# A transformer block's second-level stage: when its token operands are prepared at its start, and when the next stage's are loaded at its end

## The chip, the cores and the metric

The kernel runs on one core of a Trainium2 chip. The metric is the device time in microseconds (us) of one execution. Three executions of the kernel before took 2743.86, 2738.77 and 2740.04 us; their median is 2740.04 us.

## The reference

One sequence of 2048 tokens with 1024 features goes through an adaLN-conditioned block. Cut to its skeleton (all data is fp32):

```python
mod = (silu(c) @ w_mod) -> sa, ca, ga, sb, cb, gb      # 1024 values each
h = layernorm(x) * (1 + ca) + sa
x1 = x + ga * (infini_attention(h) @ wo)               # 32 heads, 4 segments of 512 tokens
h2 = layernorm(x1) * (1 + cb) + sb
out = x1 + gb * ((gelu(h2 @ w_gate) * (h2 @ w_up)) @ w_down)   # 1024 -> 3584 -> 1024
```

The change concerns the way from `x1` through `h2` into the two products `h2 @ w_gate` and `h2 @ w_up`.

## The kernel before

**Arithmetic.** TensorE multiplies fp32 data as pairs of rounded numbers: every operand is cut into a high part `hi` (copied by ScalarE, line 925) and a low part `lo = src - hi` (VectorE or GpSimd, line 922), and every product is three matmuls: hi by hi, hi by lo, lo by hi. One such cut of an operand therefore takes one instruction on ScalarE and one on VectorE, or one on ScalarE and two half-size ones on GpSimd.

**The feed-forward stages.** The two wide products are computed with two levels of Strassen-Winograd. The level that the change touches is the *second-level stage*, `two(n)` (from L1104, matmuls in L1123). It runs over 14 weight pairs, n = 0 to 13, which the text calls pair 0 to pair 13. For each pair it computes seven products, in the order `ROUND = (1, 6, 2, 7, 5, 4, 3)`, for i = 1 and for i = 2, which are the first and the second half of the 1024 features (called the first and the second half below). A product is six matmuls of 128 by 512, a pair 84. The products add up in PSUM in tiles `pa` (products 1 and 2), `pb` (6, 7, 4) and `pc` (5, 3); `pa` shares two PSUM buffers, and `pb` and `pc` share five. The evictions are `c<-pa` on ScalarE (L1133), `x<-pb`, `x<-pc` on VectorE for i = 1 and `y<-pb`, `y<-pc` for i = 2 (L1139, L1141), and GpSimd adds x to y. Pair 0 runs the seven products of i = 1 and then the seven of i = 2; all other pairs alternate i = 1 and i = 2 for each product. The results go to a DRAM tensor `st_d`, from which the next stage reads them back.

That next stage is `gate_up(m)` (L1350, 60 matmuls for each m): five more products for each of 28 chunks of the 3584 columns in a first pass over half of the tokens (m = 0 to 27) and in a second pass over the other half (m = 28 to 55). Its token operands `A{pass}_{product}_{kt}` are prepared by `a_next(p)` (L1180): ten loads `ra` of 512 KB each, two to a product, and four cuts to a product.

**Token operands of the second-level stage.** They are called `AA{i}_{r}_{c}`: half i, product r, chunk c (0 or 1). They come from `unit(i, c, p)`, a load `u` of 512 KB from the normalised tokens `h_d`, with p the group of tokens (p = 0 is segment 0, p = 1 is segment 2). `a_early` loads the units (1, 0, 0) and (1, 1, 0) early and prepares AA1_1 and AA1_2. `a_first` then waits until segment 2 is normalised, loads everything else, and prepares the rest: for each i, sums and differences of the units (s, u: L1016 to L1018 on VectorE, the difference `diff` on GpSimd), and then a cut for each product and chunk. For products 5 and 4 with c = 1, the low part is computed on GpSimd, for all others on VectorE. `a_first` loads the units (1, 0, 0) and (1, 1, 0) a second time, because `a_early` does not hand its tiles on. The units (2, 1, p) go to tiles of the T ring, which exists only once the projections' pools are closed (`pools(3)`); in the build the loads `units(2, 1)` are therefore issued when the last projections are done.

**What runs ahead of it.** The attention's output projection (L773, eviction `xr<-y` on VectorE, L777) runs in blocks of four token tiles; the last two, block (3,0) and block (3,1), stand right before pair 0. Between the matmuls of block (3,0) TensorE transposes segment 2's normalised tokens (L269, `tpb<-ident,nb`), four tiles of 128 tokens, two steps for each. `norm_steps` spaces these: for four token tiles or fewer, a tile's statistics come 4 steps after its load, its scaling (L248 on ScalarE) after 6 and its transposes after 9, and a new tile starts every 4 steps.

**Order and queues.** For TensorE, VectorE, ScalarE and GpSimd the order in this part of the kernel is that of the program: generators ("sides") are stepped between the products, so each engine's instructions stand in the order in which the code issues them, and each engine works through its list in that order. SyncE (SP) issues nearly all DMAs, in an order set by a scheduler, and it too works in order: a DMA that waits for its buffer holds up those behind it.

**Rings in SBUF that matter.** `raw` has 4 buffers (weights of a pair, units, g and u weights of the next stage), `ra` 2, `T` 5 (the x outputs of a pair, some units, some `ra` loads), `g` 3 (the y outputs).

**The end of the stage.** At pair 13, `a_next(0)` is started as a side: it issues five loads (three to T buffers, two to `ra` buffers), then prepares one operand after another, each after the product of pair 13 that frees the operand's place. The third and each later step first issues one more load, to an `ra` buffer. Beside it runs `b_part(0)`, which prepares the weights of m = 0. `gu_load(1)`, the weights of m = 1 (`rg1`, `ru1`), is issued after product 4 of i = 2 of pair 13. At m = 27, `a_next(1)` does the same for the second pass.

## Time and profile before

The profiled execution took 2744.0 us; its span, the time from the first to the last instruction, is 2742.3 us.

| what | us |
|---|---|
| median of three executions | 2740.04 |
| the profiled execution | 2744.0 |
| its span | 2742.3 |
| TensorE busy in the span | 2677.0 (98 %) |
| pair 0 (1121.2 to 1160.5) | 39.3 |
| pair 1 (1160.5 to 1183.3) | 22.8 |
| pair 13 (1397.9 to 1428.8) | 30.9 |
| m = 0 (1428.8 to 1449.5) | 20.7 |

In the rows of the profile, times are in us from the span's start. "DVE" is VectorE, "ACT" ScalarE, "POOL" GpSimd, "PE" TensorE, "SPq" the queue of SyncE. A row gives start, duration, engine, source line, operation, output and inputs, and in square brackets the idle time before it on its engine and what ended that. The difference between the time of a pair and that of its 84 matmuls when nothing holds them up is time in which TensorE waits or runs at a lower clock.

### The profile page before, as it was taken

The numbers are of one execution on the slowest core, as the hardware profiler recorded it, in microseconds if no ns is written. First come the engines' busy times: TensorE is split into PE (matmuls) and PEld (weight loads), VectorE is DVE, ScalarE is ACT, GpSimd is POOL, SyncE is SP. The second block draws the span as 40 slices with busy tenths as digits, with TensorE's granted clock in tenths as the row PEclk, the third lists the DMA queues.
The fourth block names the chain that finished last, engine by engine and source line by source line (L and its number), as shares of the span: only waits on it lengthen the run. The fifth ranks groups of instructions, "written<-read, shape, count | busy, mean of one in ns | idle before, by whom it ended". The sixth has DMA issues, their size and how long they took to land.

```text
span 2742.3 us, 42592 instructions
## 1 busy us (share of the span) xinstructions
PE 2677.0 (98%) x14068; PEld 2227.6 (81%) x14068; DVE 1753.4 (64%) x3746; ACT 1261.3 (46%) x2924; POOL 1066.2 (39%) x1646
## 2 busy tenths in 40 slices
PE   7999999999999999899989999999999999999999
PEld 6898888888888787678867888878888888888887
DVE  7677667776766745577766655567666654575456
ACT  6778776767676634354442222232222233233323
POOL 4333334433333532365648777736565300000000
PEclk9999999999999999899999999999999999999999
DMA  7455535444434577366769988789999897795563
GB/s 261 112 158 143 134 113 162 120 129 141 131 101 135 175 236 234 125 219 208 249 210 356 335 276 270 264 287 370 370 373 367 332 332 237 262 307 198 183 207 125
DMA packets 266188, 613.37 MB, mean 224 GB/s; under 512 B 26992, under 2 KB 51568, under 8 KB 265968
## 3 DMA queue, kind: packets, MB, share of 16 engines
q1 hardware_dynamic: 265968, 610.66, 66.7%
q8 instruction: 111, 1.82, 0.3%
q14 instruction: 109, 0.89, 0.1%
HBM read 372.53 MB, written 187.70 MB: 204 GB/s over the span
## 4 chain that ended last, share of the span: by engine, by line
PE 52%; DMA 3%; DVE 3%; POOL 1%; issue 1%; ACT 1%; SPq 0%; DVEq 0%; POOLq 0%; ACTq 0%
PE f L1350 25%; PE y L1550 19%; PE pb L1123 3%; PE pc L1123 2%; PE pa L1123 2%; DMA rm<-h_d 1%; DVE A L922 1%; DMA ra<-mix_d 1%; DMA X<-hid_d 0%; DMA u<-h_d 0%; DMA wr<-gd_d 0%; POOL y L922 0%; DMA ru<-wu 0%; DVE AA L922 0%; DMA mix_d<-rm 0%
## 5 line engine op out<-in xcount | busy, mean ns | idle before, releaser
L1350 PE MATMUL f<-A,B 128*128 128x512 f32 x3360 | 766.0, 391 | 8.9 <-ACT B L925 3.8
L1350 PEld LDWEIGHTS f<-A,B 128*128 128x128 f32 x3360 | 631.7, 188 | 142.8 <-ACT B L925 6.8
L1550 PE MATMUL y<-B,L 128*128 128x512 f32 x2352 | 533.9, 390 | 0.6 <-DVE L L922 0.3
L1550 PEld LDWEIGHTS y<-B,L 128*128 128x128 f32 x2352 | 441.6, 188 | 92.6 <-ACT L L925 0.7
L611 ACT ACTIVATE sj<-sj,mm 128x384 f32<-128x384 f32 (+3 forms) x512 | 281.1, 552 | 40.2 <-DVE mm L609 39.6
L698 POOL TENSOR_SCALAR_AFFINE_SELECT pt<-pt 128x128 f32<-128x128 f32 x512 | 166.8, 347 | 332.3 <-ACT pt L697 324.3
L609 DVE CUSTOM_DVE_ANT_0 sj<-S,mask 128x384 f32<-128x384 f32 (+3 forms) x512 | 228.2, 488 | 97.0 <-PE S L607 70.7
L697 ACT ACTIVATE pt<-T 128x256 f32<-128x256 f32 (+3 forms) x512 | 182.3, 444 | 132.4 <-PE T L695 126.0
L1376 ACT ACTIVATE g<-g 128x512 f32<-128x512 f32 x56 | 35.4, 633 | 415.7 <-DVE g L1375 402.1
L925 ACT ACTIVATE L<-X 128x512 fp32r<-128x512 f32 x168 | 105.8, 630 | 257.3 <-PE y L1550 165.6
L922 DVE TENSOR_TENSOR L<-X,L 128x512 fp32r<-128x512 f32 x168 | 115.9, 691 | 145.7 <-ACT L L925 145.7
L386 POOL TENSOR_TENSOR w<-r,w 128x256 fp32r<-128x256 f32 x180 | 133.2, 771 | 141.5 <-ACT w L380 141.5
L395 PE MATMUL kv<-w,hha 128*128 128x256 f32 x896 | 175.2, 287 | 2.2 <-DVE vx L413 2.2
L1264 POOL TENSOR_TENSOR rw<-rw,gbb 128x256 f32<-128x256 f32 x112 | 109.2, 1009 | 155.9 <-DMA rw<-wd 150.6
L1123 PE MATMUL pb<-AA,BB 128*128 128x512 f32 x504 | 129.9, 406 | 20.2 <-DVE x L1139 15.4
L395 PEld LDWEIGHTS kv<-w,hha 128*128 128x128 f32 x896 | 145.3, 193 | 3.4 <-DVE vx L413 2.5
L1123 PEld LDWEIGHTS pb<-AA,BB 128*128 128x128 f32 x504 | 97.5, 196 | 44.5 <-DVE x L1139 18.0
L773 PE MATMUL y<-wo,hho 128*128 128x512 f32 x384 | 127.8, 396 | 0.2 <-DVE xr L777 0.2
L395 PE MATMUL kv<-w,hla 128*128 128x256 f32 x448 | 127.5, 285 | 0.0
L695 PE MATMUL T<-qs,ks 128*128 128x256 f32 (+3 forms) x512 | 105.7, 327 | 1.8 <-DVE ry L674 1.1
L607 PE MATMUL S<-ks,qs 96*128 96x384 f32 (+3 forms) x512 | 106.9, 330 | 0.3
L925 ACT ACTIVATE B<-t 128x512 fp32r<-128x512 f32 x84 | 49.7, 622 | 121.4 <-POOL t L922 121.4
(283 smaller groups left out, 5179.2 us busy)
## 6 DMA issues: line engine op xcount, KB each, us to landing
B<-wc_d SPq DMA_DIRECT2D x112, 512.0 KB, 3.4
cg<-st_d SPq DMA_DIRECT2D x112, 256.0 KB, 6.6
hid_d<-g SPq DMA_DIRECT2D x56, 512.0 KB, 4.5
wc_d<-T SPq DMA_DIRECT2D x56, 512.0 KB, 6.5
X<-hid_d SPq DMA_DIRECT2D x112, 256.0 KB, 4.9
bc_d<-B SPq DMA_DIRECT2D x54, 512.0 KB, 6.1
B<-bc_d SPq DMA_DIRECT2D x54, 512.0 KB, 7.1
wr<-gd_d SPq DMA_DIRECT2D x84, 256.0 KB, 4.1
```

The lines of the kernel that those rows point to most:

```text
L386: nc.gpsimd.tensor_sub(w[:, 1, c], r[:, c], f32(w[:, 0, c]))
L395: nc.tensor.matmul(ps, b[:, sl], w[:, a], start=(kt == 0 and a == 0 and b is hi), stop=(kt == KT - 1 and a == 1), **kw)
L609: nc.vector.tensor_tensor_reduce(out=sj[:, :nv], in0=ps[:, :nv], in1=mask[:, L - nv:], scale=-1.0, scalar=3.4e38, op0=ALU.add, op1=ALU.min ...
L611: nc.scalar.activation(sj[:, :nv], sj[:, :nv], AF.Exp, bias=mm[:, j, i:i + 1], scale=-1.0, accum_out=ll[:, i, j:j + 1])
L697: nc.scalar.activation(pt, ps[:, nn - n:nn], AF.Exp)
L698: nc.gpsimd.affine_select(pt[:, :P], pt[:, :P], pattern=[[1, P]], compare_op=ALU.is_ge, fill=0.0, base=0, channel_multiplier=-1)
L773: nc.tensor.matmul(ps, b[:, i * P:(i + 1) * P], w[:, a, g % 2], start=(g == 0 and a == 0 and b is hi), stop=(g == G - 1 and a == 1))
L922: f(*xs)
L925: nc.scalar.activation(hi, src, AF.Copy)
L1123: nc.tensor.matmul(ps, w[:, a, at:at + P], A["a", i, r, k][b], start=(r in (1, 6, 5) and k == a == b == 0), stop=(k == 1 and a == 1), skip ...
L1350: nc.tensor.matmul(ps, B[m, i][:, a, kt * P:(kt + 1) * P], A[p, i, kt][b], start=(start and kt == 0 and a == 0 and b == 0), stop=(kt == 3 ...
L1550: nc.tensor.matmul(banks[t], ops[k][:, y, t * P:(t + 1) * P], B[slots[k]][:, x], start=(i not in (2, 4, 3) and j == 0 and x == 0 and y == ...
```

## The change

It has five parts.

1. **`norm_steps`** for four tiles or fewer (segment 2 alone): statistics, scaling and transposes come 6, 8 and 13 steps after the load, before 4, 6 and 9.
2. **The early units are kept.** `a_early` stores its tiles in `ts`, and `a_first` uses them: two loads of 512 KB less.
3. **Order in `a_first`.** Before, it went through half 1, and then through half 2 with both chunks of each product together. Now, after half 1, it prepares chunk 0 of half 2 alone; chunk 1 waits until product 4 of i = 1 of pair 0 has been issued (`ff["half"]`). The difference of units (2, 1, p) moves from GpSimd to VectorE.
4. **Exit.** `a_next(0)` starts at pair 12, before at pair 13, with seven loads ahead, before five; the sixth and seventh go to `raw` buffers, the last three to T buffers. It is also stepped ahead of `b_part(0)`. `gu_load(1)` is issued from `a_next` at its eighth operand.
5. **Pass boundary.** In `a_next(1)`, five steps pass ahead of the ninth operand, the first of product 4.

```diff
-        period, at_stat, at_scale, at_turn = (5, 5, 7, 10) if len(toks) > 4 else (4, 4, 6, 9)
+        period, at_stat, at_scale, at_turn = (5, 5, 7, 10) if len(toks) > 4 else (4, 6, 8, 13)
...
-            ts = [unit(1, c, 0, raw_tile) for c in range(2)]
+            for c in range(2):
+                ts[1, c] = [unit(1, c, 0, raw_tile)]
...
             for c in range(2):
-                units(1, c)
-            units(2, 0)
+                ts[1, c].append(unit(1, c, 1, raw_tile))
+            units(0, ra_tile)
...
+            for c in range(2):
+                summed(1, c)
+                yield
+            for r in (6, 7, 5, 4, 3):
+                for c in range(2):
+                    put(1, r, c)
                     yield
...
+            put(2, 1, 0)
+            yield
+            summed(2, 0)
+            yield
+            for r in ROUND[1:]:
+                if r == 5:
+                    while (2, 1) not in ts:
                         yield
+                put(2, r, 0)
+                yield
+            while not ff.get("half"):
+                yield
+            put(2, 1, 1)
+            yield
+            summed(2, 1, nc.vector)
+            yield
+            for r in ROUND[1:]:
+                put(2, r, 1)
+                yield
...
+                if n == 0 and (i, r) == (1, 4):
+                    ff["half"] = True
...
-                    gu_load(1)
...
+            T_tile = lambda n: pair_tile(n, "T", 5)
+            homes = [T_tile] * 3 + [ra_tile] * 2 + [raw_tile] * 2 + [T_tile] * 3 if p == 0 else (
+                [raw_tile] * 2 + [ra_tile]) * 3 + [raw_tile]
...
-            for _ in range(5):
+            for _ in range(5 if p else 7):
                 load()
...
-                if q > 1:
+                if q > p:
                     load()
+                if p == 0 and q == 7:
+                    gu_load(1)
                 while (("a", 2, ROUND[q // 2]) if p == 0 else (FC - 1, i)) not in done:
+                    yield
+                for _ in range(5 if (p, q) == (1, 8) else 0):
                     yield
...
-        units(2, 1)
+        units(1, lambda n: pair_tile(n, "T", 5))
...
             elif n:
+                sides.append([b_part(0), 1, "b"])
+            if n == NJ - 2:
                 flush("m")
                 following = a_next(0)
-                sides.append([b_part(0), 1, "b"])
                 sides.append([following, 2])
```

**VectorE at the start of the stage.** In these rows `xr2<-y3_1_k` are the evictions of the last projection block's tiles, `AA` the low parts of the token operands, `u2_1_0` the unit of half 2 and chunk 1, and `x0_1<-pb0_1` the first eviction of pair 0. Before:

```order
L777 TENSOR_TENSOR xr2_14586<-y3_1_1_14658,xr2_14586 128x512
L1033 TENSOR_TENSOR u1_1_0_14607<-u1_1_0_14607 128x512
L922 TENSOR_TENSOR AA1_3_1_1_14714<-u1_1_0_14607,AA1_3_1_0_14713 128x512
L777 TENSOR_TENSOR xr2_14586<-y3_1_2_14718,xr2_14586 128x512
L777 TENSOR_TENSOR xr2_14586<-y3_1_3_14745,xr2_14586 128x512
L922 TENSOR_TENSOR AA2_1_0_1_14796<-u2_0_0_14611,AA2_1_0_0_14795 128x512
L922 TENSOR_TENSOR AA2_1_1_1_14800<-u2_1_0_14779,AA2_1_1_0_14799 128x512
L1139 TENSOR_TENSOR x0_1_14793<-pb0_1_14803,c0_1_14791 128x512
```

And now:

```order
L922 TENSOR_TENSOR AA1_3_1_1_14710<-u1_1_0_14295,AA1_3_1_0_14709 128x512
L922 TENSOR_TENSOR AA2_1_0_1_14714<-u2_0_0_14607,AA2_1_0_0_14713 128x512
L1013 TENSOR_TENSOR s1_2_0_14725<-u2_0_1_14609 128x512
L1015 TENSOR_TENSOR u2_0_0_14607<-s1_2_0_14725,u2_0_0_14607 128x512
L922 TENSOR_TENSOR AA2_6_0_1_14731<-u2_0_0_14607,AA2_6_0_0_14730 128x512
L922 TENSOR_TENSOR AA2_2_0_1_14741<-u2_0_0_14607,AA2_2_0_0_14740 128x512
L922 TENSOR_TENSOR AA2_7_0_1_14745<-u2_0_1_14609,AA2_7_0_0_14744 128x512
L777 TENSOR_TENSOR xr2_14586<-y3_1_2_14718,xr2_14586 128x512
L777 TENSOR_TENSOR xr2_14586<-y3_1_3_14762,xr2_14586 128x512
L922 TENSOR_TENSOR AA2_5_0_1_14813<-s1_2_0_14725,AA2_5_0_0_14812 128x512
L922 TENSOR_TENSOR AA2_4_0_1_14817<-u2_0_1_14609,AA2_4_0_0_14816 128x512
L1156 TENSOR_TENSOR x0_1_14810<-pb0_1_14820,c0_1_14808 128x512
```

Six instructions on chunk 0 of half 2 now stand ahead of the evictions of the projection's third and fourth tile, and the low part of chunk 1, AA2_1_1, no longer stands ahead of pair 0's first eviction.

**SP at the end of the stage.** Here `ra0_{product}_{b}` are the loads of `a_next(0)`, and `st_d` the stores of the pairs' outputs (x12 is an x output of pair 12). Before:

```order
L1150 DMA st_d0_74<-x12_1_17020 128x512
L1150 DMA st_d1_75<-y12_0_17039 128x512
L1194 DMA ra0_6_0_17187<-mix_d0_70 128x2x512
L1194 DMA ra0_6_1_17189<-mix_d0_70 128x2x512
L1194 DMA ra0_5_0_17191<-mix_d0_70 128x2x512
L1194 DMA ra0_5_1_17193<-mix_d0_70 128x2x512
L1194 DMA ra0_7_0_17195<-mix_d0_70 128x2x512
L1150 DMA st_d0_74<-y12_1_17040 128x512
L1194 DMA ra0_7_1_17248<-mix_d0_70 128x2x512
L1194 DMA ra0_3_0_17269<-mix_d0_70 128x2x512
L1150 DMA st_d0_74<-x13_0_17178 128x512
L1194 DMA ra0_3_1_17292<-mix_d0_70 128x2x512
```

And now:

```order
L1167 DMA st_d1_75<-y11_0_16868 128x512
L1212 DMA ra0_6_0_17026<-mix_d0_70 128x2x512
L1212 DMA ra0_6_1_17028<-mix_d0_70 128x2x512
L1212 DMA ra0_5_0_17030<-mix_d0_70 128x2x512
L1212 DMA ra0_5_1_17032<-mix_d0_70 128x2x512
L1212 DMA ra0_7_0_17034<-mix_d0_70 128x2x512
L1212 DMA ra0_7_1_17036<-mix_d0_70 128x2x512
L1212 DMA ra0_3_0_17038<-mix_d0_70 128x2x512
L1167 DMA st_d0_74<-y11_1_16869 128x512
L1167 DMA st_d0_74<-x12_0_17014 128x512
L1167 DMA st_d0_74<-y12_0_17048 128x512
L1167 DMA st_d1_75<-x12_1_17015 128x512
```

Seven loads now stand between the stores of pair 11 instead of five behind those of pair 12; nine stores of pairs 11 and 12 stand behind them, until `ra0_3_1`.

**VectorE at the pass boundary.** `c0_28<-f0_28` is the first eviction of m = 28, `A1_4` the second pass's operands of product 4. Before:

```order
L1375 TENSOR_TENSOR g27_20559<-f0_27_20555,cg27_0_20335 128x512
L922 TENSOR_TENSOR A1_4_0_1_20714<-ra1_4_0_20663,A1_4_0_0_20713 128x512
L922 TENSOR_TENSOR A1_4_1_1_20718<-ra1_4_0_20663,A1_4_1_0_20717 128x512
L1377 TENSOR_TENSOR g27_20559<-g27_20559,c1_27_20558 128x512
L922 TENSOR_TENSOR A1_4_2_1_20745<-ra1_4_1_20681,A1_4_2_0_20744 128x512
L922 TENSOR_TENSOR A1_4_3_1_20749<-ra1_4_1_20681,A1_4_3_0_20748 128x512
L1362 TENSOR_TENSOR c0_28_20727<-f0_28_20725,cg28_0_20444 128x512
```

And now:

```order
L1397 TENSOR_TENSOR g27_20554<-f0_27_20550,cg27_0_20330 128x512
L1399 TENSOR_TENSOR g27_20554<-g27_20554,c1_27_20553 128x512
L1384 TENSOR_TENSOR c0_28_20714<-f0_28_20712,cg28_0_20439 128x512
L922 TENSOR_TENSOR A1_4_0_1_20739<-ra1_4_0_20658,A1_4_0_0_20738 128x512
L922 TENSOR_TENSOR A1_4_1_1_20751<-ra1_4_0_20658,A1_4_1_0_20750 128x512
L922 TENSOR_TENSOR A1_4_2_1_20755<-ra1_4_1_20676,A1_4_2_0_20754 128x512
L1387 TENSOR_TENSOR c1_28_20715<-f1_28_20713,cg28_0_20439 128x512
```

The four cuts of product 4 now stand behind the first eviction of m = 28, three of them ahead of its second eviction.

More of the change, by code (lines that the diff above doesn't have):

```diff
@@ L979, in normed @@
             return all(stored.get(("bc"[s == 3], s)) == 8 for s in segs)
+        ts = {}
         def a_early():
@@ L989, in a_early, with units @@
                 for c in range(2):
-                    put_two(1, r, c, ts[c][:, k], nc.vector)
+                    put_two(1, r, c, ts[1, c][0][:, k], nc.vector)
                     yield
-        get = {1: [(raw_tile, raw_tile)] * 2, 2: [(ra_tile, ra_tile), (lambda n: pair_tile(n, "T", 5),) * 2]}
-        ts = {}
-        def units(i, c):
-            ts[i, c] = [unit(i, c, p, get[i][c][p]) for p in range(2)]
+        def units(c, get):
+            ts[2, c] = [unit(2, c, p, get) for p in range(2)]
         def a_first():
```

45 lines of the change are left out of this document (17 added, 28 removed).

## The prediction

> **What bounds the kernel now.** I read the page first, then the waits of TensorE, then busy times by windows, then the chain of waits and the timelines at the places found. The page:
>
> ```profile
> span 2742.3 us, 42592 instructions
> PE 2677.0 (98%) x14068; PEld 2227.6 (81%) x14068; DVE 1753.4 (64%) x3746; ACT 1261.3 (46%) x2924; POOL 1066.2 (39%) x1646
> ```
>
> TensorE is busy 98 % of the span, so what the others do counts only where TensorE waits. Its waits (us in all, times, longest) that bear on this change:
>
> ```profile
> PE pb L1123 <- DVE x L1139: 15.4, 6, 5.6
> PE tpb L269 <- ACT nb L248: 6.0, 4, 1.6
> ```
>
> The first lies in the second-level stage, the second in the transposes ahead of it. By windows (span, busy time of PE, PEld, DVE, ACT and POOL, granted clock, DMA share, GB/s):
>
> ```profile
> 1068.00:1099.45 31.45, 25.44 (x126) 20.08 (x125) 16.22 (x44) 10.98 (x20) 2.19 (x4) 1.00 0.59 172
> 1121.20:1160.50 39.30, 27.04 (x87) 20.88 (x86) 21.81 (x32) 13.31 (x23) 13.30 (x15) 0.78 0.35 121
> 1160.50:1183.30 22.80, 20.17 (x86) 15.33 (x85) 15.95 (x23) 10.84 (x20) 15.36 (x19) 1.00 0.42 139
> 1397.90:1428.80 30.90, 23.31 (x85) 17.28 (x85) 20.18 (x30) 16.18 (x30) 15.20 (x18) 0.89 0.68 220
> 1428.80:1449.50 20.70, 15.64 (x62) 12.26 (x61) 10.76 (x16) 5.70 (x10) 12.54 (x17) 0.92 1.03 374
> ```
>
> They are the last transposes, pair 0, pair 1, pair 13 and m = 0. The price of an undisturbed matmul is in the chain of waits, in pair 2:
>
> ```profile
> 1187.08 2.72 PE pb L1123 x12
> ```
>
> 2.72 / 12 = 0.227 us, so 84 matmuls take 19.0 us and the 60 of m = 0 13.6. Pair 0 loses 39.3 - 19.0 = 20.3, pair 1 3.8, pair 13 11.9, m = 0 7.1: 43 us in all, at both ends of the stage. No edit removes a matmul; the change can only take from these losses, the 6.0 of the transposes, and one wait at the pass boundary.
>
> **Entry: pair 0 before.** TensorE's timeline:
>
> ```profile
> 1121.43 1.52 PE L1123 MATMUL pa<-AA,BB 128*128 128x512 f32 x6
> 1131.22 2.93 PE L1123 MATMUL pb<-AA,BB 128*128 128x512 f32 x6 [5.55 <-DVE x L1139]
> 1138.90 2.93 PE L1123 MATMUL pb<-AA,BB 128*128 128x512 f32 x6 [3.32 <-DVE x L1139]
> 1151.92 2.93 PE L1123 MATMUL pb<-AA,BB 128*128 128x512 f32 x6 [3.38 <-DVE y L1139]
> 1168.69 1.66 PE L1123 MATMUL pa<-AA,BB 128*128 128x512 f32 x6 [0.63 <-ACT c L1133]
> ```
>
> Gaps come between products, and after each of over 3.3 us six matmuls take 2.93 instead of 1.52: half the clock. VectorE explains the first gap:
>
> ```profile
> 1100.65 0.69 DVE L1016 TENSOR_TENSOR s<-u 128x512 f32<-128x512 f32 x1 [0.62 <-DMA u<-h_d]
> 1104.26 0.69 DVE L1016 TENSOR_TENSOR s<-u 128x512 f32<-128x512 f32 x1 [0.68 <-DMA u<-h_d]
> 1106.63 0.69 DVE L1018 TENSOR_TENSOR u<-s,u 128x512 f32<-128x512 f32 x1 [1.68 <-POOL u L922]
> 1108.44 1.89 DVE L922 TENSOR_TENSOR AA<-u,AA 128x512 fp32r<-128x512 f32 x3
> 1114.46 0.69 DVE L922 TENSOR_TENSOR AA<-u,AA 128x512 fp32r<-128x512 f32 x1 [0.70 <-ACT AA L925]
> 1115.07 0.68 DVE L777 TENSOR_TENSOR xr<-y,xr 128x512 f32<-128x512 f32 x1
> 1129.88 0.69 DVE L922 TENSOR_TENSOR AA<-u,AA 128x512 fp32r<-128x512 f32 x1 [5.05 <-ACT AA L925]
> 1130.49 0.68 DVE L1139 TENSOR_TENSOR x<-pb,c 128x512 f32<-128x512 f32 x1
> ```
>
> The eviction x<-pb at 1130.49 stands behind the cut at 1129.88 (AA2_1_1), which waits through ScalarE for a load that the chain shows landing at 1129.20:
>
> ```profile
> 1124.82 4.38 DMA u<-h_d
> ```
>
> **Entry: what changes.** The eviction now comes ahead of AA2_1_1, so half 1 should run through. Against that, the work on chunk 0 of half 2 now stands ahead of the last projection evictions, and these free the two PSUM buffers that pair 0's pa needs. I follow VectorE. The second s started 3.61 after the first (1104.26 - 1100.65), with two loads of 512 KB for each; two loads instead of four halve that, 1.8. Fewer waits of the transposes (6.0 to an estimated 2.0; they move 12 matmuls, 2.7, later) leave a little more: s some 2.2 earlier, at 1102.0. From there to the end of y3_1_1's eviction VectorE needed 11.5 (1115.75 - 1104.26), now until 1113.5. Then come the rows that now stand before y3_1_2's eviction: u 0.6, AA1_3_1 with its wait for ScalarE 1.4, AA2_1_0 0.6, s 0.6, the difference on POOL 1.68, u 0.69, ScalarE 0.7 and AA2_6 0.69, AA2_2 and AA2_7 1.2, the eviction 0.6: 8.8 (0.6 is a third of the 1.89). Pair 0 starts at S = 1122.3, against 1121.43. TensorE alone, with 4.0 less of transposes' waits, would be there at 1117.4; y3_1_3's matmuls end about 3.3 us ahead of S, and a gap of about 2.7 stands before them.
>
> From S, half 1 takes 42 x 0.227 = 9.5. The loads of chunk 1 come after the pools close, as before: landing 7.8 after 1121.43, so here before half 2 needs them. Then chunk 1's cuts lead the way, and GpSimd's list:
>
> ```profile
> 1140.72 2.26 POOL L922 TENSOR_TENSOR AA<-s,AA 128x256 fp32r<-128x256 f32 x2 [4.59 <-ACT AA L925]
> 1142.94 1.94 POOL L922 TENSOR_TENSOR AA<-u,AA 128x256 fp32r<-128x256 f32 x2
> 1147.81 1.77 POOL L922 TENSOR_TENSOR t_a<-g,g 128x256 f32<-128x256 f32 x2 [2.94 <-DMA g<-wg]
> 1149.55 2.30 POOL L922 TENSOR_TENSOR t_a<-g,t_a 128x256 f32<-128x256 f32 x2
> 1158.22 1.83 POOL L922 TENSOR_TENSOR y<-y,x 128x256 f32<-128x256 f32 x2 [6.37 <-DVE y L1141]
> ```
>
> Two cuts (AA2_5_1, AA2_4_1) and two differences for pair 1's weights take 2.26 + 1.94 + 1.77 + 2.30 = 8.3. They begin when VectorE has done, after half 1's end, its last eviction and six instructions of chunk 1 (0.6 each, the difference that moves from GpSimd among them) with two waits of 0.7 for ScalarE: 5.6, at S + 15.1; so they end at S + 23.4. Pair 1's BB_6 cut waits for that on VectorE, ahead of the last pc eviction: ScalarE 0.7, cut 0.69, eviction 0.6, and POOL's first y starts at S + 25.4. Before, pair 1's pa of i = 2 (1168.69) came 10.5 after POOL's y (1158.22), so now at S + 35.9 = 1158.2: 10.5 sooner. From this go matmuls at half clock: 1.41 for a product (2.93 - 1.52), two after the gap at S, 2.8 at most for it; I take 2.5, and **-8** for the entry. Bounds: -3, if also the gap before y3_1_3 and a longer POOL chain take their price; -13, if S comes 2 us sooner at full clock.
>
> The clock deserves a sentence of its own. The row at 1138.90 shows a gap of 3.32 with half speed behind it. The Trainium skill, page "TensorE: Matmul & The Clock Gate", section "Part 1: The HAM clock gate (the "warmup" mystery)", has the clock halved only after at least one whole idle window of about 3.4 us, in windows that run freely of the kernel: by that a gap of 3.3 costs nothing, and the total below would be -26.2 instead of -23.7. By that rule, the trace disagrees at 3.32, and it decides.
>
> The two loads that go (1 MB in all) lay beside matmuls; they count only through the 1.8 above.
>
> **Exit.** TensorE in pair 13 and m = 0:
>
> ```profile
> 1407.77 1.66 PE L1123 MATMUL pb<-AA,BB 128*128 128x512 f32 x6 [1.50 <-DVE x L1139]
> 1417.81 4.43 PE L1123 MATMUL pb<-AA,BB 128*128 128x512 f32 x12 [3.78 <-DVE x L1139]
> 1445.20 7.11 PE L1350 MATMUL f<-A,B 128*128 128x512 f32 x24 [3.83 <-ACT B L925]
> ```
>
> ScalarE's first cut, the weight cut on VectorE, and SP's queue, from their timelines:
>
> ```profile
> 1405.16 1.15 ACT L925 ACTIVATE A<-ra 128x512 fp32r<-128x512 f32 x2 [3.12 <-DMA ra<-mix_d]
> ```
>
> ```profile
> 1396.09 0.69 DVE L922 TENSOR_TENSOR BB<-g,BB 128x512 fp32r<-128x512 f32 x1 [1.37 <-ACT BB L925]
> ```
>
> ```profile
> 1400.56 2.54 SPq L1194 DMA_DIRECT2D ra<-mix_d  x5
> ```
>
> And in the chain of waits a load of m = 1's weights:
>
> ```profile
> 1432.47 7.12 DMA ru<-wu
> ```
>
> Five ra loads are issued at 1400.56, inside pair 13 (1397.9 on); ScalarE's first cut waits 3.12 for them, VectorE stands behind it with pair 13's evictions. The late ru load (landing 1439.59) delays m = 1's weights, which share engines with m = 0's. Now the seven loads stand before pair 12's stores. Six can be issued in pair 12, around 1381 to 1385 (pair 12 starts 19 us ahead of 1397.9); the seventh, ra0_3_0, goes to a raw buffer whose last reader is pair 13's weight cut, BB at 1396.09 to 1396.78, so SP stands there, with nine stores behind it, until 1396.8. Those stores hold T and g buffers that pair 13 needs from about 1406 on; 9 us are enough for 9 x 256 KB (2.3 MB at the window's 374 GB/s: 6.3). No cut waits for a load; then VectorE's own work is the limit: 20.18 in the window of pair 13, against TensorE's 19.0. With the first eviction 3 us after its start, pair 13 takes 20.2 + 3 = 23.2 and ends at 1421. Of m = 0's 7.1, the 3.83 goes if ru1 is issued at about 1415 rather than after the bc_d stores; I leave it 1 us of gap: 13.6 + 1 = 14.6, end at 1435.6 against 1449.5, -13.9. I take **-13.5**. Bounds: -16.5 (pair 13 at 20.2, no gap in m = 0), -8 (ru1 late again: +3.8, and 1.5 more in pair 13).
>
> **Pass boundary.** Its rows:
>
> ```profile
> 1823.60 1.29 DVE L922 TENSOR_TENSOR A<-ra,A 128x512 fp32r<-128x512 f32 x2 [1.22 <-ACT A L925]
> 1826.62 0.68 DVE L1362 TENSOR_TENSOR c<-f,cg 128x512 f32<-128x512 f32 x1
> 1827.44 8.90 PE L1350 MATMUL f<-A,B 128*128 128x512 f32 x38 [2.23 <-DVE c L1362]
> ```
>
> The eviction of m = 28 stood behind A1_4's cuts; now it is ahead of them, and product 4, four products on (48 matmuls, 10.9), hides the cuts, 4 x 1.2. **-2.2**, between 0 (the wait returns at the next eviction, c1_28, behind three cuts) and -2.2.
>
> **The sum.** -8 - 13.5 - 2.2 = -23.7. The profiled execution took 2744.0, so 2720.3; it lies 4.0 above the median of the runs shown, 2740.04, and on that the forecast is 2740.04 - 23.7 = 2716.3.
>
> **The rivals.** *A, entry spent on the POOL chain:* GpSimd's 8.3 start later or grow beside VectorE, and pair 1 comes only 3 sooner, half 1's gain given back in half 2. For: POOL had gaps of 4.59 and 6.37 that ended with others' work, so it hangs on chains. Against: those gaps are slack. About -16 in all, 2724. *B, VectorE not late:* the u loads come sooner and S is about 1117.4, 5 sooner, at full clock: -8 - 5 - 2.5, -31 in all, 2709. For: 4.0 of transposes' waits go; against: 8.8 of new rows. *C, exit half won:* T buffers or ru1 hold it at -7: -17, 2723. *The page's clock:* no half speed after gaps under 3.4 us: -26.2, 2713.8; the row at 3.32 is against it. *D, slower:* SP's wait at ra0_3_0, 12.3 us (1396.8 - 1384.5), passes to TensorE through the stores behind it. It decides if the last of those nine land after about 1406, when pair 13 wants their buffers. Then +12.3, the exit's gain gone, ru at its full 7.1 late, against the entry and boundary's 10.2: +9.2, 2749. For: nine stores behind one load; against: 9 us of cover. *E, nothing acts:* the waits move to the next instruction on VectorE, 2740.
>
> **How the numbers follow.** Forecast 0.50, A 0.17, C 0.11, B 0.10, the page's clock 0.05, D 0.04, E 0.03. A measurement of this kernel can tell about 0.2 % (5.5 us) from no change: faster takes all but D and E, 0.93; same 0.03; slower 0.04. Range: the best bounds together, -13 - 16.5 - 2.2 = -31.7, and B give 2708 to 2709; the worst, -3 - 8 - 0 = -11, 2729. I take 2707 to 2729; D, E and some tails stay out.
>
> **What would show it.** Right: no wait x<-pb of over 1 us in half 1 of pair 0; first matmul of pair 0 near 1122; pair 1's pa of i = 2 near 1158; ra issues before 1386, one waiting to about 1397; pair 13 near 23 us, m = 0 near 14.6; no gap of 2 us in m = 28. Wrong: pair 0 still at 35 us or more, SP's stores ending a wait of TensorE in pair 13, or ru ending a wait in m = 0.

## The result, and the profile after

The changed kernel takes 2722.39 us (median of 4 runs, 2721.36 to 2725.75) against 2740.67 for the kernel before (4 runs); the ratio is 0.9934, 95 % interval 0.9917 to 0.9951. That is 18.3 us less; the forecast was 23.7 less (2716.3, range 2707 to 2729). The profiled spans differ by the same 18.3:

```profile
span 2724.0 us, 42592 instructions
PE 2672.9 (98%) x14068; PEld 2223.2 (82%) x14068; DVE 1752.6 (64%) x3747; ACT 1260.2 (46%) x2924; POOL 1066.6 (39%) x1644
```

To see where they came from, I took the start of the first matmul of each stage from TensorE's timeline of both traces and subtracted. "Entry" runs from the first matmul of the output projection (y<-wo) to the first of pair 2.

| stage | before | after | difference | forecast |
|---|---|---|---|---|
| start to the output projection | 910.90 | 912.40 | +1.50 | 0 |
| entry | 272.72 | 263.41 | -9.31 | -8 |
| pairs 2 to 12 | 214.33 | 214.05 | -0.28 | 0 |
| pair 13 | 30.88 | 25.80 | -5.08 | -7.7 |
| m = 0 | 20.59 | 15.02 | -5.57 | -6.1 |
| m = 1 | 14.82 | 17.56 | +2.74 | 0 |
| m = 28 | 16.12 | 13.60 | -2.52 | -2.2 |
| all the rest | 1261.92 | 1262.17 | +0.25 | 0 |
| span | 2742.28 | 2724.01 | -18.27 | -23.7 |

(The forecast took 13.9 off pair 13 and m = 0 together and entered 13.5; the column splits its 13.9 in the two lengths that it gave, 23.2 and 14.6.) The first row is not the change: in the fourteen traces of this study that stretch, which no edit touches, ends between 906.98 and 912.40. A span therefore carries some 2 us of chance either way, and stages are compared rather than spans.

The waits of TensorE in the changed kernel that answer to those shown of before:

```profile
PE pb L1140 <- DVE x L1156: 4.7, 3, 3.3
PE pa L1140 <- DVE xr L777: 2.9, 1, 2.9
PE y L773 <- DVE xr L777: 2.6, 1, 2.6
PE pb L1140 <- DVE y L1156: 2.5, 4, 1.2
PE f L1372 <- DVE c L1390: 2.1, 1, 2.1
PE tpb L269 <- ACT nb L248: 1.5, 2, 1.1
```

The 15.4 of pb on x is 4.7, the 6.0 of the transposes 1.5. Three waits are new: 2.6 and 2.9 for evictions of the projection, and 2.1 in m = 1, which the forecast had not. Of the first two it had the sizes (2.7 and 3.3), but the 2.7 before y3_1_3; it came one tile sooner, before y3_1_2. The windows of pair 0, pair 1, pair 13, m = 0 and m = 1 (columns as before):

```profile
1125.30:1152.20 26.90, 22.29 (x84) 16.73 (x85) 18.02 (x28) 10.80 (x18) 8.47 (x10) 0.94 0.56 186
1152.20:1175.80 23.60, 20.63 (x89) 15.74 (x88) 16.19 (x24) 11.59 (x20) 16.16 (x20) 1.00 0.40 134
1389.80:1415.70 25.90, 22.48 (x86) 17.62 (x86) 22.33 (x32) 15.32 (x29) 16.63 (x18) 0.87 0.83 284
1415.70:1430.70 15.00, 14.14 (x62) 11.09 (x61) 8.63 (x12) 5.25 (x9) 11.80 (x16) 1.00 0.96 340
1430.70:1448.20 17.50, 15.41 (x61) 12.30 (x60) 11.44 (x13) 4.21 (x7) 17.01 (x21) 0.90 0.93 319
```

Pair 0 took 39.3 and takes 26.9. In pair 13 VectorE is busy 22.33 of 25.90 us, where it was 20.18 of 30.90, and in m = 0 8.63 where it was 10.76. One cut and one eviction more now fall into pair 13, whose window holds 18 of the 20 cuts and held 17.

**Entry.** TensorE's timeline, from the wait before y3_1_2 to pair 1's product 2 of i = 2 (1168.69 before):

```profile
1109.53 0.79 PE L773 MATMUL y<-wo,hho 128*128 128x512 f32 x1 [2.62 <-DVE xr L777]
...
1125.39 2.05 PE L1140 MATMUL pa<-AA,BB 128*128 128x512 f32 x6 [2.90 <-DVE xr L777]
1127.23 2.77 PE L1140 MATMUL pb<-AA,BB 128*128 128x512 f32 x6
...
1131.23 1.54 PE L1140 MATMUL pb<-AA,BB 128*128 128x512 f32 x6
...
1161.21 1.65 PE L1140 MATMUL pa<-AA,BB 128*128 128x512 f32 x6 [0.60 <-ACT c L1150]
```

The gap of 5.55 in half 1 is gone: products follow each other from 1125.39 to the end of half 1. Pair 0 starts at 1125.39, not at 1122.3; 1.50 of that is the later start of the trace, so counted from the first matmul of the output projection it is 212.99 instead of the forecast's 211.4 (before: 210.53). VectorE shows why:

```profile
1102.31 0.69 DVE L1013 TENSOR_TENSOR s<-u 128x512 f32<-128x512 f32 x1 [5.54 <-DMA u<-h_d]
1104.60 0.69 DVE L1015 TENSOR_TENSOR u<-s,u 128x512 f32<-128x512 f32 x1 [1.60 <-POOL u L922]
1105.21 0.68 DVE L1013 TENSOR_TENSOR s<-u 128x512 f32<-128x512 f32 x1
...
1116.01 0.68 DVE L777 TENSOR_TENSOR xr<-y,xr 128x512 f32<-128x512 f32 x1
...
1124.65 1.28 DVE L777 TENSOR_TENSOR xr<-y,xr 128x512 f32<-128x512 f32 x2
...
1135.53 0.69 DVE L1156 TENSOR_TENSOR x<-pb,c 128x512 f32<-128x512 f32 x1 [0.67 <-PE pb L1140]
```

On the same count the first s starts at 189.91, no sooner than before (189.75). The second follows 2.90 behind it, where the forecast had 1.8: u stands between the two and waits 1.60 for GpSimd's difference. So the second s comes at 192.81, the forecast had it at 191.1 (1102.0). From y3_1_1's eviction (ends 1116.69) to y3_1_2's (ends about 1125.3) it is 8.6, forecast 8.8. SP's queue shows what holds the units back:

```profile
1092.17 2.90 SPq L279 DMA_DIRECT2D h_d<-htb  x4
1097.77 0.36 SPq L975 DMA_DIRECT2D u<-h_d  x1
```

The last four stores of transposed tokens now go out together, and by the chain of waits the last took 4.11 to land, where it took 2.30 before. It is issued 1.6 sooner than before on the count from the projection, but takes 1.8 longer to land; the unit's load waits for it.

**Exit.** The seven loads in SP's queue:

```profile
1374.55 14.54 SPq L1212 DMA_DIRECT2D ra<-mix_d  x7
```

They go out in pair 12, and the last of them holds SP until 1389.09, 0.8 us ahead of pair 13, as the forecast had it (1396.8 with pair 13 at 1397.9). No wait of TensorE ends on a store behind them. Pair 13 on TensorE and VectorE:

```profile
1407.34 5.49 PE L1140 MATMUL pb<-AA,BB 128*128 128x512 f32 x12 [3.25 <-DVE x L1156]
```

```profile
1394.50 2.09 DVE L922 TENSOR_TENSOR A<-ra,A 128x512 fp32r<-128x512 f32 x2 [3.41 <-ACT A L925]
...
1406.61 0.68 DVE L1156 TENSOR_TENSOR x<-pb,c 128x512 f32<-128x512 f32 x1
```

After 3.41 us of waiting for the first cut VectorE works without a pause, and TensorE waits 3.25 in the middle of the pair for an eviction that stands behind ten cuts. And m = 1:

```profile
1441.87 1.21 DVE L959 TENSOR_TENSOR m<-rm,rm 128x512 f32<-128x512 f32 x1 [4.10 <-DMA rm<-h_d]
1443.01 0.68 DVE L1390 TENSOR_TENSOR c<-f,c 128x512 f32<-128x512 f32 x1
```

```profile
1443.83 2.41 PE L1372 MATMUL f<-A,B 128*128 128x512 f32 x5 [2.09 <-DVE c L1390]
```

Here the mixing of the second pass's tokens (`a_mix(1)`, L959) waits on VectorE for a load, and m = 1's eviction stands behind it. The same wait was there before, 2.97 us, and it cost TensorE 0.93:

```profile
1459.47 1.18 DVE L959 TENSOR_TENSOR m<-rm,rm 128x512 f32<-128x512 f32 x1 [2.97 <-DMA rm<-h_d]
```

```profile
1461.40 3.91 PE L1350 MATMUL f<-A,B 128*128 128x512 f32 x16 [0.93 <-DVE c L1368]
```

Before, the loads rm were issued 1.41 us after the first matmul of m = 1 (1450.83 - 1449.42), now 2.81 after it (1433.49 - 1430.68); they take as long to land (8.6 and 8.4). Why they go out later in m = 1 was not tested.

**Boundary.** TensorE's timeline from 1799.78 has no gap through the start of m = 28 (1803.63):

```profile
1799.78 32.58 PE L1372 MATMUL f<-A,B 128*128 128x512 f32 x143
```

### The profile page after: what moved, and what is told of

It is laid out like the page before. It is cut to its first block, busy times and chain, and to the rows that moved or that the text cites. A ratio compares the mean times of both kernels' runs of the same rounds, so it can differ in the third digit from the quotient of the medians.

```text
span 2724.0 us, 42592 instructions
## 1 busy us (share of the span) xinstructions
PE 2672.9 (98%) x14068; PEld 2223.2 (82%) x14068; DVE 1752.6 (64%) x3747; ACT 1260.2 (46%) x2924; POOL 1066.6 (39%) x1644
## 4 chain that ended last, share of the span: by engine, by line
PE 89%; DVE 3%; DMA 2%; issue 2%; ACT 1%; POOL 1%; SPq 0%; DVEq 0%; POOLq 0%; ACTq 0%
PE f L1372 27%; PE y L1572 19%; PE kv L395 9%; PE q L401 6%; PE y L773 5%; PE pb L1140 3%; PE S L607 3%; PE T L695 3%; PE O L707 3%; PE pa L1140 2%; PE pc L1140 2%; PE kT L514 2%; PE vT L514 2%; PE num L663 1%; PE M L646 1%
```

## The experiments

Stages were read as in the table above. Each ratio is to runs of the kernel before on the same chip.

| kernel | median us (before) | ratio, 95 % interval | entry | pair 13 | m = 0 | m = 1 | m = 28 |
|---|---|---|---|---|---|---|---|
| before | | | 272.72 | 30.88 | 20.59 | 14.82 | 16.12 |
| changed | 2722.39 (2740.67) | 0.9934, 0.9917-0.9951 | 263.41 | 25.80 | 15.02 | 17.56 | 13.60 |
| entry_only | 2735.61 (2743.45) | 0.9970, 0.9961-0.9979 | 263.70 | 29.61 | 20.90 | 15.09 | 17.74 |
| exit_only | 2731.14 (2743.45) | 0.9954, 0.9939-0.9969 | 273.38 | 25.53 | 15.29 | 15.29 | 13.60 |
| spacing_back | 2725.59 (2742.32) | 0.9939, 0.9923-0.9956 | 264.97 | 25.53 | 15.26 | 17.48 | 13.60 |
| gu_back | 2720.91 (2742.32) | 0.9922, 0.9908-0.9937 | 262.68 | 25.54 | 15.27 | 18.27 | 13.60 |
| mix_later | 2719.68 (2743.45) | 0.9914, 0.9896-0.9932 | 263.74 | 25.52 | 15.27 | 13.66 | 13.60 |
| chunk0_late | 2723.48 (2743.45) | 0.9931, 0.9916-0.9946 | 264.54 | 25.54 | 15.28 | 18.24 | 13.60 |
| sums_late | 2723.13 (2745.05) | 0.9920, 0.9906-0.9935 | 261.57 | 25.50 | 15.14 | 17.55 | 13.60 |
| chunk0_late_sums_late | 2717.72 (2742.32) | 0.9912, 0.9897-0.9926 | 260.23 | 25.54 | 15.26 | 16.02 | 13.60 |
| slow_cuts | 2735.84 (2742.32) | 0.9974, 0.9964-0.9983 | 263.98 | 19.79 | 25.96 | 25.11 | 13.60 |
| slow_cuts_early_weights | 2713.67 (2743.65) | 0.9898, 0.9881-0.9914 | 259.31 | 19.77 | 22.28 | 13.60 | 13.60 |
| hold_two | 2715.55 (2745.05) | 0.9896, 0.9879-0.9913 | 258.92 | 25.52 | 14.84 | 13.60 | 13.59 |
| hold_four_no_pool | 2716.30 (2745.05) | 0.9898, 0.9883-0.9913 | 259.03 | 26.78 | 17.19 | 13.60 | 13.60 |

Five traces have the changed kernel's code at the entry (changed, entry_only, gu_back, mix_later, slow_cuts). Their entries lie between 262.68 and 263.98, but pair 0 starts in all of them 212.94 to 213.00 after the first projection matmul. So differences of under 1.3 us between entries, their spread, are not read; those of pair 0's start are.

**entry_only**: parts 4 and 5 undone, that is `homes`, seven loads, the append at pair 12, the place of `gu_load(1)` and the five steps of the boundary.

```diff
-            for _ in range(5 if p else 7):
+            for _ in range(5):
                 load()
...
-            if n == NJ - 2:
                 flush("m")
                 following = a_next(0)
```

> The changed kernel with its parts 4 and 5 (exit, pass boundary) undone; parts 1 to 3 stay. Theory: the parts add up, and the entry is worth what the traces show between the start of the last projections and pair 13: first matmul of pair 0 near 1125, pair 2 about 8 us sooner than before, then the old pair 13 (30.9 us), m = 0 (20.7) and m = 28 (16.1). Expected 8 us less than before, 2732 to 2733. Rival: the entry's gain only shows because the exit is shorter too, since the late loads of pair 13 wait for something that does not move; then pair 13 gets longer by what was won, and the time is that of before, 2740.

The entry is worth what it is in the changed kernel, 272.72 - 263.70 = 9.0, and the old exit is back (29.61, 20.90, 15.09). In time it is a ratio of 0.9970, 8.2 us of 2743.45. The rival falls: pair 13 does not take the gain back. (m = 28 takes 17.74 here and 16.12 in the kernel before, with the same code; the last section comes back to it.)

**exit_only**: the same edits of parts 4 and 5, on the kernel before.

> The kernel before with parts 4 and 5 alone. Theory: pair 13 about 25.8 us instead of 30.9, m = 0 15.0 instead of 20.6, m = 1 17.6 instead of 14.8, m = 28 13.6 instead of 16.1, as in the changed kernel: 5.1 + 5.6 - 2.7 + 2.5 = 10.5 us less than before, 2730. Rival (from the forecast, which gave the exit 13.5 and the boundary 2.2): m = 1's new wait belongs to the meeting of both ends of the stage, and alone the exit gives 13 or more: 2726 or below.

Pair 13, m = 0 and m = 28 come out as in the changed kernel; m = 1 takes 15.29, not 17.56. Its new wait is smaller here (the eviction c is waited for 1.4 instead of 2.1 us). The time, 0.46 % or 12.6 us of 2743.45, lies between theory (10.5) and rival (13 and more), and by the interval (8.5 to 16.7) settles nothing; by the traces the three stages give 10.2 and the boundary 2.5, 12.7 in all. So the exit alone is worth 10.2, some 2.3 more than in the changed kernel (7.9), and all of that difference is m = 1. There the rows lean to the rival: m = 1 is 0.47 longer than before, not 2.7.

**spacing_back**: part 1 undone.

```diff
-        period, at_stat, at_scale, at_turn = (5, 5, 7, 10) if len(toks) > 4 else (4, 6, 8, 13)
+        period, at_stat, at_scale, at_turn = (5, 5, 7, 10) if len(toks) > 4 else (4, 4, 6, 9)
```

> The changed kernel with part 1 undone (statistics, scaling and transposes of segment 2 again 4, 6 and 9 steps behind the load). Theory: the transposes' waits return (1.5 to about 6 us), but pair 0's start hangs on VectorE, which waits for the units behind the last transposed tile's store; that store moves by 2 us at most, and the wait of 2.6 us before y3_1_2 shrinks by as much. Expected 0 to 2 us slower than the changed kernel. Rival: TensorE's waits count in full: 4.5 us slower.

Its waits of TensorE:

```profile
PE tpb L269 <- ACT nb L248: 6.0, 4, 1.6
PE pa L1140 <- DVE xr L777: 2.9, 1, 2.9
PE y L773 <- DVE xr L777: 0.7, 1, 0.7
```

The transposes wait 4.5 us more, and pair 0 starts only 1.05 later (214.03 against 212.99; the entry is 1.6 longer). The wait of 2.6 before y3_1_2 is gone, and with it the half clock behind it, by which y3_1_2's 24 matmuls took 7.2 in the changed kernel (1109.53 to 1116.75) instead of 5.4; 0.7 is left, before y3_1_3. The theory holds: most of what the spacing won on TensorE was lost again at the next eviction, which hangs on VectorE.

**gu_back**: only the place of `gu_load(1)` as before.

```diff
-                if p == 0 and q == 7:
-                    gu_load(1)
...
                         cg_load(q)
+                    gu_load(1)
```

> The changed kernel with the load of m = 1's weights (rg1, ru1) again issued behind product 4 of i = 2 of pair 13, and not at the eighth operand. Theory (the forecast's step): ru1 then lands late behind the stores, and a wait of 3 to 4 us comes back in m = 0 or m = 1: 3 to 4 us slower than the changed kernel. Rival: with the stage's end sooner by the other parts the load is early enough either way, or GpSimd is the one that is late: within 1 us of the changed kernel.

The rival holds: m = 0 takes 15.27 with the load at its old place, and 15.02 with the move. The moved load has nothing to do with the 3.83 that m = 0 lost. What fits it is the order in SP's queue, of the kernel before and then of gu_back:

```profile
1413.72 3.82 SPq L1194 DMA_DIRECT2D ra<-mix_d  x2
...
1426.41 0.36 SPq L1194 DMA_DIRECT2D ra<-h_d  x1
...
1428.40 3.56 SPq L1217 DMA_DIRECT2D cg<-st_d  x4
1432.00 0.43 SPq L1223 DMA_DIRECT2D rg<-wg  x1
1432.47 0.43 SPq L1223 DMA_DIRECT2D ru<-wu  x1
```

```profile
1396.22 2.70 SPq L1213 DMA_DIRECT2D ra<-h_d  x2
...
1411.42 0.37 SPq L1244 DMA_DIRECT2D ru<-wu  x1
```

Before, SP issued the last ra loads at 1413.72 to 1426.77, each when the cuts freed a buffer, and so ru 3.6 us after m = 0 began (1428.83). With the ra loads done early it passes ru 1.1 us before m = 0 (1412.54) from the place that it had before. GpSimd's first instruction on m = 1's weights waited 3.35 for ru before (1439.75); in gu_back it starts at 1419.45 without a wait. No run moves the ra loads alone, so this is read from rows.

**mix_later**: the mixing's first use of a load stands eight steps behind it.

```diff
-                for _ in range(4):
+                for _ in range(4 if p == 0 else 8):
                     yield
                 a11, a21, a12, a22 = r[0][:, :h], r[0][:, h:], r[1][:, :h], r[1][:, h:]
```

> The changed kernel; in the mixing of the second pass's tokens (a_mix(1)) eight steps pass between a load rm and its first use, instead of four. Theory: m = 1's new wait (2.09 us, and half clock behind it) comes from VectorE standing at m<-rm,rm for 4.10 us until the load lands, with m = 1's eviction behind it; with eight steps m = 1 takes 14 to 15 us instead of 17.6, and the time falls by 2.5 to 3.5 us. Rival: m = 1 waits for its weights, prepared late on GpSimd (17.0 of 17.5 us busy there); then m = 1 stays at 17 us or the wait moves into m = 2.

```profile
1428.68 21.65 PE L1372 MATMUL f<-A,B 128*128 128x512 f32 x94 [0.74 <-ACT B L925]
```

m = 1 runs without a gap in 13.66, 3.9 less, while GpSimd is busy all through it (13.70 of 13.70 us from 1431.50 on), so it is not the weights. The wait in m = 1 is the mixing's, as the theory had it. The trace decides this; the interval of the time overlaps that of the changed kernel.

**chunk0_late**: chunk 0 of half 2 waits until the last projections are done.

```diff
+            while (2, 1) not in ts:
+                yield
             put(2, 1, 0)
             yield
             summed(2, 0)
             yield
             for r in ROUND[1:]:
-                if r == 5:
-                    while (2, 1) not in ts:
-                        yield
                 put(2, r, 0)
```

> The changed kernel, with the chunk 0 operands of half 2 not prepared before the projection's last evictions, but after them, between pair 0's evictions. Theory: they made pair 0's start late; now y3_1_2 is evicted right behind AA1_3_1, and pair 0 starts when y3_1_3's matmuls end, near 1122.3 instead of 1125.4, 3 us sooner. VectorE has some 9 more rows of 0.6 us to do in half 1, so 1 to 2 us of it are lost again behind half 1; the total 1 to 3 us below the changed kernel. Rival: the work is due either way, and the chain of VectorE and GpSimd behind pair 0 starts no sooner; pair 0 is longer by what its start gains, 0 us; or the rows hold up half 1's evictions, and gaps of over 1 us before pb come back (slower).

```profile
1118.02 1.52 PE L1139 MATMUL pa<-AA,BB 128*128 128x512 f32 x6
...
1124.89 2.93 PE L1139 MATMUL pb<-AA,BB 128*128 128x512 f32 x6 [2.63 <-DVE x L1155]
```

From the first projection matmul pair 0 starts 3.15 sooner (209.84 against 212.99), as predicted, and is 4.6 longer (31.45 against 26.83): a gap is back in half 1, with half clock behind it, because pair 0's first eviction stands behind chunk 0's sums. The entry as a whole is 1.1 longer, within the spread. The rival holds: the start of pair 0 is not what the entry's length hangs on.

**sums_late** and **chunk0_late_sums_late**: the sums come later, so that y3_1_0's eviction stands ahead of them; alone, and with the edit of chunk0_late.

```diff
             units(0, ra_tile)
-            for _ in range(3):
+            for _ in range(7):
                 yield
```

> The changed kernel, with seven steps instead of three between a_first's loads and its sums, alone; chunk 0 of half 2 stays ahead of the last evictions. It tells which of the two edits of chunk0_late_sums_late made the start of the stage 3.2 us shorter (from the first projection matmul to pair 2), where chunk0_late alone made it 1.1 longer. Theory: the wait of 2.6 us before y3_1_2 goes, but y3_1_2's own eviction still stands behind VectorE's list, which starts at the units' landing as before and has one eviction less and two cuts less ahead (0.6 + 1.2 us): pair 0 starts 1.8 us sooner, and that stays: -1.8 us. Rival: both edits are needed, and alone it gives 0 (VectorE sets the start either way). Third: it gives the 3.2 alone.

> As chunk0_late, and a_first waits seven steps instead of three behind its loads, so that the eviction of y3_1_0 stands ahead of the sums on VectorE, which wait 5.5 us for their units. Theory: the 2.6 us wait before y3_1_2 goes, and TensorE gets to pair 0 without a gap, near 1117.8 instead of 1125.4. Pair 0's half 1 then runs ahead of VectorE, which has the same work to do as before; of the 7.6 us some 4 to 5 stay: 4 to 5 us below the changed kernel. Rival: the end of the entry is set by VectorE and GpSimd from the landing of the units on, whatever stands in front: no more than chunk0_late alone.

Alone, the entry is 1.84 shorter, as the theory said (the interval of the ratio, 0.9906 to 0.9935, cannot tell that from the changed kernel). With both edits it is 3.2 shorter, under the 4 to 5 expected: pair 0 starts 6.9 sooner and is 3.4 longer. By the entries, later rows of chunk 0 cost 1.1 without the sums' delay and win 1.3 with it; both lie within the spread, so whether the one edit depends on the other was not settled.

**slow_cuts** and **slow_cuts_early_weights**: one cut instead of two for each product of pair 13; the second has `gu_load(1)` at its old place, mix_later and the entry of hold_two.

```diff
             if n == NJ - 2:
                 flush("m")
                 following = a_next(0)
-                sides.append([following, 2])
+                sides.append([following, 1])
```

> The changed kernel; the first pass's operands are stepped once for each product of pair 13 instead of twice, so that some 12 instead of 20 cuts stand in pair 13 and the rest in m = 0. Theory: pair 13 (25.8 us) is bound by VectorE (22.3 us busy there and 3.4 us of one wait); 8 cuts of 0.6 us less make it 4 us shorter, of which m = 0 gives back 1 to 2: 2 to 4 us less than the changed kernel. Rival: cuts that are late hold up m = 0, which waits for A0_7 and then A0_3 and A0_4; then what pair 13 gains m = 0 loses, 0 us or slower.

> slow_cuts mixed two things: one cut for each product of pair 13, and, since gu_load(1) hangs on the eighth operand, m = 1's weights loaded only in m = 0. Here the cuts are slow, the weights' load stands behind product 4 of i = 2 of pair 13 again, a_mix(1) waits eight steps, and the entry is that of hold_two. Theory: pair 13 is 19.8 us as in slow_cuts; m = 0 keeps the wait of 6.1 us for an eviction behind late cuts and some 2.7 of half clock: about 22.4; m = 1 about 14. Pair 13 to m = 1 take 56, 2 us more than in hold_two (54.0). Rival: the waits in m = 0 came from the late weights too; then m = 0 takes 15 to 17 and the three 49 to 51, 3 to 5 us less than hold_two.

Pair 13 falls to 19.8, 0.8 above its 84 matmuls, with nine cuts in its window instead of 18, so the cuts are what made it long. But m = 0 and m = 1 lose more than that. In slow_cuts part of it was a fault of the experiment: `gu_load(1)` hangs on the eighth operand, which now comes so late that m = 1's weights were loaded twice, the second ru at 1424.94, 17.3 us into m = 0, and the chain of waits leads from that load into m = 1. The second kernel is free of that, and gives 19.77, 22.28 and 13.60, 55.65 in all, against the theory's 56 and the rival's 49 to 51. Its m = 0:

```profile
1400.03 5.61 PE L1370 MATMUL f<-A,B 128*128 128x512 f32 x24
1411.87 30.32 PE L1370 MATMUL f<-A,B 128*128 128x512 f32 x123 [6.22 <-DVE c L1382]
```

```profile
1410.38 0.75 DVE L922 TENSOR_TENSOR A<-ra,A 128x512 fp32r<-128x512 f32 x1 [2.48 <-ACT A L925]
1411.05 0.68 DVE L1382 TENSOR_TENSOR c<-f,cg 128x512 f32<-128x512 f32 x1
```

Five cuts that pair 13 no longer holds stand ahead of m = 0's first eviction, and three of them wait 1.9 to 2.5 us for ScalarE. What pair 13 gains, m = 0 gives back.

**hold_two** and **hold_four_no_pool**: the entry of chunk0_late_sums_late with the difference of units (2, 0) on VectorE, the weights' load at its old place, mix_later, and the last four (A0_4) or eight cuts (A0_3, A0_4) held until m = 0; the second also moves the cuts AA2_5_1 and AA2_4_1 from GpSimd to VectorE.

```diff
+                while p == 0 and q >= 8 and not ff.get("first_m"):
+                    yield
                 for k in range(2):
                     put_a(p, i, 2 * b + k, rs[q][:, k], nc.vector)
```

> The changed kernel with, at the entry, chunk0_late_sums_late and the difference of units (2, 0) on VectorE instead of GpSimd; at the exit, mix_later, gu_load(1) at its old place, and the last four of the 20 cuts (A0_4) held until m = 0. Theory: at the entry a wait of 1.5 us for GpSimd goes that stands ahead of pair 0's first eviction: 1 to 1.5 us less than chunk0_late_sums_late. At the exit 4 x 0.6 us less on VectorE in pair 13: 25.5 to some 23.5; m = 0 15.3 or up to 1 more, m = 1 13.7. In all 8 to 10 us below the changed kernel: ratio to before about 0.990. Rival: the exit's end is set by GpSimd's sums of y (their gelu stands ahead of cuts on ScalarE); then m = 0 loses what pair 13 wins.

> As hold_two, with two differences. Entry: the cuts AA2_5_1 and AA2_4_1 go from GpSimd to VectorE. If GpSimd's chain (two cuts, 4.2 us, then pair 1's two differences) sets the end of the entry, as the forecast had it, the wait for BB_6 (2.2 us) and the next ones shrink: 1.5 to 2.5 us less than hold_two from pair 0 to pair 2. If VectorE does, the 1.2 us of cuts more on it make it up to 1 us longer. Exit: the last eight cuts (A0_3, A0_4) are held until m = 0. If VectorE's work sets pair 13, it is 2.4 us shorter again, 21 to 22 us; A0_3 is due 8.2 us into m = 0, and if ScalarE reaches it late, m = 0 takes 2 to 4 us longer than in hold_two.

The exit's theory fails in both: pair 13 takes 25.52 and 26.78 with 16 and 12 cuts in it. hold_two's TensorE shows the same gap as the changed kernel at the same place of the pair:

```profile
1401.51 4.41 PE L1139 MATMUL pb<-AA,BB 128*128 128x512 f32 x12 [3.23 <-DVE x L1155]
...
1408.06 1.66 PE L1139 MATMUL pc<-AA,BB 128*128 128x512 f32 x6 [0.75 <-DVE y L1157]
```

On VectorE, the first cut of the pair and the eviction that ends the second wait:

```profile
1388.67 2.09 DVE L922 TENSOR_TENSOR A<-ra,A 128x512 fp32r<-128x512 f32 x2 [3.41 <-ACT A L925]
...
1407.33 0.68 DVE L1157 TENSOR_TENSOR y<-pc,y 128x512 f32<-128x512 f32 x1
```

The first eviction stands behind the first ten cuts (A0_6, A0_5, half of A0_7), not the last ones. The second, y<-pc, for which the pair's last product waits, stands behind sixteen, at the end of 19.3 us in which VectorE works without a pause (1388.67 to 1408.01); the four cuts that are held stood behind it.

In hold_four_no_pool VectorE waits for TensorE at the end of the pair (0.63, 1.87 and 0.94), and TensorE runs its last 18 matmuls at half clock (granted clock 0.57 from 1403.90 to 1410.90), which costs about 2.9: six take 2.93 and twelve 4.39, instead of 1.52 and 2.88. That execution is also 2.7 us longer than the next of its kernel, so its 26.78 may be in part chance. With the eight held, m = 0 is late as well (17.19; waits for ScalarE's cuts and for weights).

At the entry, hold_two is 1.3 shorter than chunk0_late_sums_late, the size of the theory, but no more than the spread, and pair 0, where it was to come, is as long (30.28 against 30.25). With GpSimd's two cuts on VectorE the entry changes by 0.1: the 1.5 to 2.5 that GpSimd's chain was to give do not come; the loss of up to 1, if VectorE set the end, could not be told from the spread. (Pair 0 is 1.1 shorter and pair 1 1.0 longer, but so they are in slow_cuts_early_weights, which has hold_two's entry.) What sets the entry's end was not settled.

hold_two, hold_four_no_pool and slow_cuts_early_weights are all some 0.99 of the kernel before, by the ratio 28 us less, and faster than the changed kernel; their intervals do not part them. hold_two's ratio is what was expected, 0.990, but it comes from the entry and m = 1, not from pair 13.

Parts 2 and 3 of the change were not run apart, so how the entry's gain divides between the kept units and the new order is not known.

## Why the prediction was right, and where it was off

The direction, the places and the order of size were right: three parts, each a gain, and no slowdown from SP's queue. Of 23.7 us came 18.3; the exit is what fell short.

1. **Entry, forecast -8, measured -9.3.** That half 1 runs through was right. Pair 0's start was off by 1.6 (212.99 against 211.4). The step that failed is "two loads instead of four halve that, 1.8": it took the sums to be bound by the number of loads. The first s waits for the last transposes' stores and comes no sooner than before, and the second follows 2.90 behind it, because VectorE waits for GpSimd's difference in between. From the start of pair 0 on, the sum was 35.9 to pair 1's product 2, and 2.5 for half clock on top; measured are 35.8 in all (1161.21 - 1125.39). Two errors inside it cancel. GpSimd's two cuts and two differences began 16.3 after pair 0's start, not 15.1: matmuls at half clock (2.05 and 2.77 instead of 1.52 each, 1.8) held up half 1, and two of its evictions waited 0.67 each for TensorE (one is the row at 1135.53 above). But they took 7.0, not 8.3, so that they ended 23.3 after it, for 23.4. So the number of the entry is near by luck: +1.6 at the start against -2.5 for the clock. That the chain is GpSimd's was argued from rows; hold_four_no_pool speaks against it.
2. **Transposes.** 6.0 to "an estimated 2.0" became 1.5; that this does not reach pair 0, since VectorE is late, is shown by spacing_back: 4.5 of waits are worth 1.05 at pair 0's start.
3. **Exit, forecast -13.5, measured -7.9.** Two steps failed. First, pair 13, 25.8 where 23.2 was forecast. "VectorE's own work is the limit: 20.18" took the work of the old window; one cut and one eviction more fall into the new one, and it is 22.33, with a wait of 3.41 where 3 was assumed: 25.7. But that sum does not explain the length: hold_two has two cuts fewer in pair 13, VectorE is as busy there with evictions that had lain in m = 0, and the pair takes 25.52. What the runs show is the order on VectorE: the evictions for which TensorE waits (3.25 in the middle of the pair) stand behind ten and sixteen cuts. In the changed kernel's trace the half clock behind that gap comes on top (granted clock 0.87 in the pair); in exit_only it does not, TensorE waits instead, and the pair takes 25.53. Second, m = 1 was put at no change. VectorE's wait for rm, which stands ahead of m = 1's eviction, cost TensorE 0.93 before and costs 2.09 now, and 1.7 of half clock behind it. mix_later shows this: without the wait m = 1 is 3.9 us shorter. m = 0 came out near the forecast (15.02, forecast 14.6). That an early ru ends the wait fits the rows; that the load had to be moved for it was wrong: gu_back has it back at its place and m = 0 at 15.27.
4. **SP's wait** was forecast to end 1.1 us ahead of pair 13, ended 0.8 ahead, and cost nothing; rival D falls.
5. **Boundary, forecast -2.2, measured -2.52**; every kernel with this part shows the same 13.60. What it saves depends on the clock behind the old gap: against entry_only's 17.74 it would be 4.1.
6. **Rivals.** C (half the exit's gain) is nearest to what happened, at -7.9 for -7, by another cause than the two it named. A and B did not come about, nor did the fifth rival, no half speed after gaps under 3.4 us: it followed gaps of 2.62, 2.90 and 3.25.

## What to carry to other kernels

When loads and cuts are moved ahead, count the work of the engine that does them in the stage where it will now lie, not where the old profile showed it, and look at what stands in that engine's queue one stage further: a wait that cost little before can grow when the stage ends sooner. Cuts spread over two stages only shifted the wait here, since evictions stood behind them on the same engine. A gain on the busiest engine ahead of a stage is worth only what the chain into that stage leaves: 4.5 us of waits were worth 1.05.

## What was not expected of the hardware

The granted clock behind a gap does not follow from the gap's length. Behind the 2.09 us in m = 1 it fell to 0.52 (window 1443.8 to 1446.6), and twelve matmuls took 4.4 us instead of 2.7; behind the 2.23 us at the boundary of the kernel before it stayed at 1.00:

```profile
1443.80:1446.60 2.80, 2.77 (x7) 2.22 (x8) 2.77 (x4) 0.00 (x0) 2.79 (x3) 0.52 1.05 370
```

```profile
1827.40:1830.00 2.60, 2.56 (x11) 2.15 (x12) 0.49 (x1) 0.00 (x0) 0.00 (x0) 1.00 0.95 318
```

In entry_only, whose code there is the same, the same gap of 2.23 us (before 1818.12) was followed by half clock, and m = 28 took 17.74 instead of 16.12:

```profile
1819.70:1823.00 3.30, 3.30 (x10) 2.56 (x9) 0.65 (x1) 0.00 (x0) 0.00 (x0) 0.50 0.99 366
```

The Trainium skill, page "TensorE: Matmul & The Clock Gate", section "Part 1: The HAM clock gate (the "warmup" mystery)", has the windows run freely of the kernel, which agrees with one length and two outcomes; that a whole window of about 3.4 us must be idle, these 2.09 us and the 2.90 ahead of pair 0 do not bear out.
